# A first attention product in pairs of heads on two row groups of the matmul array

## The chip, the cores and the metric

The kernel runs on one core of a Trainium2 chip. A core has five engines that run their own instruction streams in order: TensorE (PE, matmuls, with its weight loads shown apart as PEld), VectorE (DVE), ScalarE (ACT), GpSimd (POOL) and SyncE (SP), which here issues nearly all loads and stores. Matmuls write to PSUM, eight banks of 2 KB a partition; the other data lie in SBUF, 128 partitions wide. The metric is the device time of one execution in microseconds (us). Before the change it is 344.74 us, the median of three runs (344.7 to 345.59).

## The reference: what is computed

Inputs are q, k, v and an output gate (4 batches, 8 heads, 768 steps, head size 40), an input and a forget gate (4, 8, 768), and weights of a feed-forward block. The first part is a recurrence over time with a decaying state:

```python
for t in range(S):
    m_new = np.maximum(f_gate[:, :, t] + m, i_gate[:, :, t])
    f_stab = np.exp(f_gate[:, :, t] + m - m_new)
    i_stab = np.exp(i_gate[:, :, t] - m_new)
    m = m_new
    C = f_stab[:, :, None, None] * C + i_stab[:, :, None, None] * np.einsum('bhd,bhe->bhde', vt, kt)
    n = f_stab[:, :, None] * n + i_stab[:, :, None] * kt
    h_tilde = np.einsum('bhde,bhe->bhd', C, qt)
    denom = np.maximum(np.abs(nq), 1.0)          # nq = n . q
    y[:, :, t] = o * h_tilde / denom             # o = sigmoid(o_gate)
```

The second part takes y with its heads side by side (4, 768, 320), multiplies by `w_in` (320 to 1024), applies ReLU, a convolution of width 3 over time for each of the 1024 channels, gates the result with its own sigmoid, and multiplies by `w_out` (1024 to 320). Results are f32.

## The kernel before, in words

**Tiling.** Time is cut into chunks of 128 steps: 6 a batch, 24 in all (`s`). Two chunks make a unit of 256 steps: 12 in all (`u`). Inside a chunk the recurrence is written as attention: a first product k.q for every head (128 x 128, "pS"), times a matrix of decay factors (`w`, an exp on ScalarE; `ch_p` multiplies on VectorE), then a second product with v (`ch_pv`, into "pY", 41 columns a head: 40 values and a one for the denominator). What earlier chunks hand on is a state matrix, updated by `ch_u` and `ch_state` and applied by `ch_inter`. The quotient and the gate give x (`ch_rden`, `ch_num`, `ch_x`), which is transposed on TensorE (`ch_t`) and split into a high and a low f32r part (`ch_split`, `ch_splitl`).

**Feed-forward block (FFN).** For each unit and each of 8 slices of the 1024 channels, 8 matmuls of 258 columns into "ph" (`f_m1`, line 618), ReLU, three taps, tanh and split on ScalarE, VectorE and GpSimd, and 6 matmuls of 320 columns into "po" (`f_m2`, line 681). Weights arrive as 64-bit numbers; `wabs`, `wc0` to `wc3`, `wsh` and `wsl` turn them into f32r pairs during the first part of the run.

**The first product before (`ch_s`, line 464).** Heads are kept in three groups of 3, 3 and 2, one above the other on partitions 0 to 119 (`q`, 40 a head). The stationary operand of head n is a tile `kz` of 120 partitions in which only that head's 40 are not zero; a matmul over 120 rows (80 in the last group) then gives that head's product. `kz` exists twice, is zeroed once by GpSimd (line 367), and a unit's loads (`att_kz`, lines 371 and 375) fill only the parts that are not zero: one load for q, three for k. Four heads fill one PSUM bank; the two banks of a chunk are two jobs, `s0` and `s1`. The pool `ps_m` (tag "m") has three banks, which `s0`, `s1`, `u` (state update), `t` (transposes) and the early gate transposes share in turn. The tile `q` is also read by `att_qe` on GpSimd or VectorE, which makes the operand of `ch_inter`.

**What sets the order.** Nothing is scheduled by the compiler. The kernel lists its pieces as jobs (`at(...)`) with what they come after, a cost on each engine (`COST`), a priority (place in the program plus an offset in `OFF`, `WZ`, `WL`), an earliest time for loads (`REL`, `SLOPE`), and a ring of buffers. The function `order` runs through this plan once while the program is built, always taking the job that could start first by those costs, and the jobs are written out in that order; each engine then follows its own part of it. Where the plan leaves TensorE idle early on, `warm` matmuls ("pw") fill the gap so that its clock stays up. On the chip only semaphores and the order on each engine count.

**Decay factors of the first three chunks** (`NP = 3`, `ch_gpe`, lines 405 and 408) are made on TensorE, by a 128-row matmul of 512 columns and four 32-row matmuls for each half of a chunk; later chunks load them (`ch_loadw`).

## Time and profile before

| what | before |
|---|---|
| median of three runs | 344.74 us |
| the profiled execution | 344.72 us |
| its span, first to last instruction | 342.6 us |
| TensorE busy | 328.7 us (96%) |
| weight loads busy | 322.3 us (94%) |
| VectorE busy | 262.9 us (77%) |
| ScalarE busy | 236.3 us (69%) |
| GpSimd busy | 202.7 us (59%) |
| line 464, the first product | 384 passes, 53.1 us busy, 287 ns the mean of one |
| bytes moved by DMA | 46.09 MB |
| mean granted clock of TensorE | 0.959 |

A pass of the first product lasts 287 ns, but passes overlap, so the busy time of a group is shorter than the sum of its durations: 384 passes in 53.1 us. In a timeline the distance between the starts of two groups tells what a group takes of TensorE. A line of the stretches view gives a stretch, its length, the busy time (and instructions) of each engine, the granted clock, the mean share of the 16 DMA engines that is busy, and GB/s. A waits row gives who waited for whom, in total, how often, and the longest. KB in the sizes of loads are 1024 bytes.

### The profile page before, as it was taken

To read this page: it belongs to the slowest core of one execution; us is meant where nothing else is said; L and a number is where in the kernel's file an instruction comes from. 1 tells how busy PE (TensorE), PEld (TensorE's weight loads), DVE (VectorE), ACT (ScalarE), POOL (GpSimd) and SP (SyncE) were. 2 spreads that over 40 slices of the span, in tenths; PEclk is the share of its full clock that TensorE was granted. 3 is DMA by queue.
4 is the path that set the end of the run, shared out by engine and by line. 5 is a ranking of instruction groups with operands and counts; after the bars stand their busy time and mean duration, and the time that the engine had idled before them with its cause. 6 is when DMAs were issued, how large, how long until landed. Compare 5 with 4: busy or idle time off the path is not lost.

```text
span 342.6 us, 7422 instructions
## 1 busy us (share of the span) xinstructions
PE 328.7 (96%) x2534; PEld 322.3 (94%) x2534; DVE 262.9 (77%) x598; ACT 236.3 (69%) x610; POOL 202.7 (59%) x310
## 2 busy tenths in 40 slices
PE   7699898998999999999999999999999999999995
PEld 7588898999999999999999999999999999999995
DVE  4897889999998987778489877676888768566750
ACT  2355747879988668896958786769685536577871
POOL 7369898869968647584745661746563234343341
PEclk9855599999999999999999999999999999999999
DMA  6887658686717466174315452654211001010111
GB/s 167 273 250 299 215 196 271 192 256 180 221 53 219 150 194 205 64 216 157 101 58 153 127 160 93 187 182 147 94 59 41 0 2 38 2 38 2 38 41 38
DMA packets 18575, 46.09 MB, mean 135 GB/s; under 512 B 2579, under 2 KB 6347, under 8 KB 18539
## 3 DMA queue, kind: packets, MB, share of 16 engines
q1 hardware_dynamic: 18068, 45.22, 42.4%
q8 instruction: 20, 0.33, 0.5%
q10 hardware_dynamic: 471, 0.41, 0.4%
q14 instruction: 16, 0.13, 0.1%
HBM read 41.49 MB, written 4.13 MB: 133 GB/s over the span
## 4 chain that ended last, share of the span: by engine, by line
PE 71%; DVE 11%; POOL 6%; ACT 4%; DMA 3%; issue 3%; SPq 0%; POOLq 0%; DVEq 0%; ACTq 0%
PE po L681 22%; PE ph L618 22%; PE pY L491 10%; PE pS L464 9%; PE pY L482 3%; PE pU L502 3%; PE pT L575 2%; DMA wraw<-in_w_in 1%; DVE cv L650 1%; DVE ph L650 1%; ACT w L439 1%; DMA w<-G_d 1%; PE pg L408 1%; POOL gl L209 1%; POOL w L432 1%
## 5 line engine op out<-in xcount | busy, mean ns | idle before, releaser
L209 POOL TENSOR_TENSOR gl<-cv,gh 128x512 fp32r<-128x512 f32 x48 | 62.5, 1302 | 47.4 <-ACT gh L213 40.7
L618 PE MATMUL ph<-X,wi_h 128*128 128x258 f32 x480 | 77.1, 290 | 2.2 <-DVE cv L650 1.5
L618 PEld LDWEIGHTS ph<-X,wi_h 128*128 128x128 f32 x480 | 64.6, 190 | 3.0 <-ACT ph L636 1.7
L681 PE MATMUL po<-wo_h,gh 128*128 128x320 f32 x192 | 61.5, 320 | 0.5 <-ACT ot L687 0.5
L439 ACT ACTIVATE w<-w,aT 128x128 f32<-128x128 f32 x168 | 55.1, 391 | 8.1 <-POOL w L432 8.1
L650 DVE SCALAR_TENSOR_TENSOR ph<-h,cw_sb,ph 128x256 f32<-128x256 f32 x96 | 46.1, 483 | 18.9 <-ACT ph L636 18.4
L681 PE MATMUL po<-wo_l,gh 128*128 128x320 f32 x192 | 59.3, 309 | 0.0
L681 PE MATMUL po<-wo_h,gl 128*128 128x320 f32 x192 | 59.3, 309 | 0.0
L464 PE MATMUL pS<-q,kz 120*128 120x128 f32 (+1 forms) x384 | 53.1, 287 | 4.2 <-DVE aT L306 3.1
L464 PEld LDWEIGHTS pS<-q,kz 120*128 120x128 f32 (+1 forms) x384 | 48.6, 199 | 4.6 <-DVE aT L306 3.2
L658 DVE SCALAR_TENSOR_TENSOR cv<-cv,h 128x512 f32<-128x512 f32 x48 | 40.4, 844 | 15.9 <-ACT cv L654 15.6
L628 ACT ACTIVATE h<-ph 128x258 f32<-128x258 f32 x96 | 36.5, 380 | 23.1 <-PE ph L618 21.2
L650 DVE SCALAR_TENSOR_TENSOR cv<-h,cw_sb,ph 128x256 f32<-128x256 f32 x96 | 45.1, 476 | 8.1 <-POOL gl L209 4.9
L618 PE MATMUL ph<-X,wi_l 128*128 128x258 f32 x288 | 50.3, 283 | 0.0
L491 PE MATMUL pY<-n,w 128*128 128x41 f32 x384 | 47.8, 282 | 0.0
L491 PEld LDWEIGHTS pY<-n,w 128*128 128x128 f32 x384 | 47.2, 197 | 0.2
L636 ACT ACTIVATE ph<-h,cw_sb 128x256 f32<-128x256 f32 x96 | 45.6, 475 | 1.9
L654 ACT ACTIVATE cv<-cv 128x512 f32<-128x512 f32 x48 | 30.1, 627 | 16.3 <-DVE cv L650 9.3
L618 PEld LDWEIGHTS ph<-X,wi_l 128*128 128x128 f32 x288 | 41.3, 190 | 0.0
L213 ACT ACTIVATE gh<-cv 128x512 fp32r<-128x512 f32 x48 | 30.0, 624 | 11.2 <-PE po L681 11.2
L681 PEld LDWEIGHTS po<-wo_h,gh 128*128 128x128 f32 x192 | 36.2, 188 | 0.7 <-ACT ot L687 0.7
L681 PEld LDWEIGHTS po<-wo_l,gh 128*128 128x128 f32 x192 | 36.2, 189 | 0.0
(84 smaller groups left out, 530.0 us busy)
## 6 DMA issues: line engine op xcount, KB each, us to landing
n<-in_nat SPq DMA_DIRECT2D x24, 484.0 KB
w<-G_d SPq DMA_DIRECT2D x21, 512.0 KB
q<-in_qT SPq DMA_DIRECT2D x12, 360.0 KB
out<-ot SPq DMA_DIRECT2D x24, 160.0 KB
wraw<-in_w_in SPq DMA_DIRECT2D x8, 384.0 KB
kz<-in_kT SPq DMA_DIRECT2D x24, 120.0 KB
eq<-E_d SPq DMA_DIRECT2D x24, 120.0 KB
wraw<-in_w_out SPq DMA_DIRECT2D x8, 320.0 KB
```

The source lines that it names most:

```text
L209: (nc.gpsimd if e == "POOL" else nc.vector).tensor_tensor(out=out, in0=in0, in1=in1, op=op)
L213: nc.scalar.activation(out, in_, AF.Copy)
L439: nc.scalar.activation(w[:, h, :], g, AF.Exp, bias=aT[:, c, b * 8 + h : b * 8 + h + 1])
L464: nc.tensor.matmul(pS[:, j, :], lhsT=lhsT, rhs=rhs, start=(j == 0), stop=(j == 3), skip_group_check=True)
L491: nc.tensor.matmul(pY[:, h * VW : (h + 1) * VW], lhsT=r["w"][:, n, :], rhs=v[:, DM + h * VW : DM + (h + 1) * VW], start=(c == 0 and n == 0 ...
L618: nc.tensor.matmul(ph, lhsT=a, rhs=b_, start=(i == 0), stop=(i == len(mm) - 1))
L628: nc.scalar.activation(hj, ph, AF.Relu)
L636: nc.scalar.activation(c, hk, AF.Copy, scale=wk)
L650: nc.vector.scalar_tensor_tensor(o, hk, wk, c, op0=ALU.mult, op1=ALU.add)
L654: nc.scalar.activation(cv, cv, AF.Tanh, scale=0.5)
L658: nc.vector.scalar_tensor_tensor(cv, cv, 1.0, h[:, :, 1 : 1 + UT], op0=ALU.add, op1=ALU.mult)
L681: nc.tensor.matmul(obuf[u][k], lhsT=a, rhs=b_, start=(f == 0 and i == 0), stop=(f == 7 and i == 2))
```

## The change

The first product of a chunk becomes one job `s` of eight matmuls. Two new arrays `qP` and `kP` hold q and k with heads 0 to 3 on partitions 0 to 39 and heads 4 to 7 on partitions 64 to 103 (the rows between are zeros from the host), four heads side by side along the free dimension. Matmul j of the lower half reads partitions 0 to 39 and writes bank `pS0`; matmul j of the upper half follows it, reads partitions 64 to 103 and writes bank `pS1`. The built program places the first kind as a tile of 64 rows at row 0 of the array and the second at row 64; before, all eight were tiles of 128 rows. The products are the same, over 40 rows instead of 120 of which 80 were zeros.

Loads of a unit: `k2` and `q2` (104 x 1024 each) and `q` as before (for `att_qe`), three loads instead of four, each into a ring of three tiles instead of two fixed `kz` tiles. The zeroing of `kz` and the wait of a unit's loads for the products of two units earlier go. One job takes two `m` banks, so `order` learns of a second list of users (`users2`). The table's cost of `s` is 1.15 where `s0` and `s1` had 0.86 each; `kz` keeps its cost of 1.5 and 2.2. All offsets in `OFF`, `WZ`, `WL`, `REL` and the numbers `SLOPE` and `QMAX` are different, so the whole order of the program is another.

```diff
-    cb=374.33, s0=-143.64, s1=77.22, p0=75.42, p1=778.82, inter=-156.65, pv0=139.58, pv1=72.13, rd0=-530.16,
+    cb=332.26, s=-382.2, p0=452.72, p1=1119.87, inter=28.33, pv0=86.13, pv1=-160.67, rd0=-659.34, rd1=-395.01,
...
-    ... cb={"POOL": 1.0, "DVE": 0.5}, s0={"PE": 0.86}, s1={"PE": 0.86}, p0={"DVE": 0.61}, p1={"DVE": 0.61},
+    ... cb={"POOL": 1.0, "DVE": 0.5}, s={"PE": 1.15}, p0={"DVE": 0.61}, p1={"DVE": 0.61},
...
-REL = dict(kz=-49.15, loadn=9.51, loadw=-633.44, eg=1.3)
-SLOPE = 2.41
-QMAX = 3.0
+REL = dict(kz=-326.94, loadn=22.7, loadw=-299.53, eg=5.25)
+SLOPE = 2.32
+QMAX = 2.88
...
-                        us = rings[r][k]
+                    us = list(rings[r][k]) if k >= 0 else []
+                    if j["users2"] and k >= -1:
+                        us += rings[r][k + 1]
+                    if us:
...
-    kzt = [const.tile([120, H, UT], F32, name=f"kz{k}") for k in range(2)]
-    for t in kzt:
-        nc.gpsimd.memset(t, 0.0)
-
     def att_kz(u):
-        q = sb.tile([120, 3 * UT], F32, name="q", tag="q", bufs=3)
-        nc.sync.dma_start(out=q, in_=qT[u])
-        kz = kzt[u % 2]
-        for j in range(3):
-            ng = 3 if j < 2 else 2
-            nc.sync.dma_start(
-                out=kz[40 * j : 40 * j + 40, 3 * j : 3 * j + ng, :],
-                in_=kT[u, 40 * j : 40 * j + 40, 0 : ng * UT],
-            )
-        units.setdefault(u, {}).update(kz=kz, q=q)
+        r = units.setdefault(u, {})
+        for nm, src, rows in (("k2", kP, 104), ("q2", qP, 104), ("q", qT, 120)):
+            t = sb.tile([rows, src.shape[2]], F32, name=nm, tag=nm, bufs=3)
+            nc.sync.dma_start(out=t, in_=src[u])
+            r[nm] = t
...
-    def ch_s(s, half):
+    def ch_s(s):
         u, tt = s // 2, (s % 2) * P
         r, ur = chunks[s], units[u]
-        pS = ps_m.tile([P, 4, P], F32, name="pS", tag="m")
+        for half in range(2):
+            r["s", half] = ps_m.tile([P, 4, P], F32, name=f"pS{half}", tag="m")
         for j in range(4):
-            n = 4 * half + j
-            g = n % 3
-            kk = 40 * GRP[g][1]
-            lhsT, rhs = ur["kz"][0:kk, n, tt : tt + P], ur["q"][0:kk, g * UT + tt : g * UT + tt + P]
-            nc.tensor.matmul(pS[:, j, :], lhsT=lhsT, rhs=rhs,
-                             start=(j == 0), stop=(j == 3), skip_group_check=True)
-        r["s", half] = pS
+            for half in range(2):
+                k, q = (ur[x][64 * half : 64 * half + D, j * UT + tt : j * UT + tt + P] for x in ("k2", "q2"))
+                nc.tensor.matmul(r["s", half][:, j, :], lhsT=k, rhs=q, start=(j == 0), stop=(j == 3), skip_group_check=True)
...
-        at("kz", z, [] if u < 2 else [(f"s{k}", 2 * (u - 2) + d) for d in (0, 1) for k in (0, 1)], att_kz, u, ring="q", users=ss + qe)
+        at("kz", z, (), att_kz, u, ring="q", users=ss + qe)
...
+        at("s", z, [("kz", u)] + ([("t", s - 2)] if s > 1 else []) + ([("u", s - 1 - (s - 1) // NCB)] if c else []), ch_s, s, ring="m", users=[("p0", s)], users2=[("p1", s)])
         for k in range(2):
-            at(f"s{k}", z, qk + ([("t", s - 2)] if s > 1 else []) + ([("u", s - 1 - (s - 1) // NCB)] if c else []), ch_s, s, k, ring="m", users=[(f"p{k}", s)])
-            at(f"p{k}", z, [(f"s{k}", s), ("exp", 4 * s + 2 * k), ("exp", 4 * s + 2 * k + 1)], ch_p, s, k)
+            at(f"p{k}", z, [("s", s), ("exp", 4 * s + 2 * k), ("exp", 4 * s + 2 * k + 1)], ch_p, s, k)
...
+    def pairs(x):
+        t = np.zeros((B, 3, 104, 4, UT), np.float32)
+        y = np.asarray(x)[:, HP].transpose(0, 1, 3, 2).reshape(B, H, D, 3, UT).transpose(0, 3, 2, 1, 4)
+        t[:, :, :D], t[:, :, 64:] = y[:, :, :, :4], y[:, :, :, 4:]
+        return t.reshape(B * 3, 104, 4 * UT)
```

Where the order differs, three places. First the loads on SP before the change, from the first unit's to the first `n` (the chunk's k, v and gate in natural layout):

```order
L371 DMA q<-in_qT 120x768
L375 DMA kz_107<-in_kT 40x768 x2
L375 DMA kz_107<-in_kT 40x512
L321 DMA wraw<-in_w_in 128x768
L289 DMA G_d<-Gt 32x128
L280 DMA E_d<-ft 32x128
L371 DMA q<-in_qT 120x768
L375 DMA kz_108<-in_kT 40x768 x2
L375 DMA kz_108<-in_kT 40x512
L321 DMA wraw<-in_w_in 128x768
L427 DMA n<-in_nat 128x968
```

and in the change, after the first two units' three loads each and one weight slice, up to the first `n`:

```order
L373 DMA q<-in_qT 120x768
L325 DMA wraw<-in_w_in 128x768
L382 DMA eq<-E_d 40x768 x2
L382 DMA eq<-E_d 40x512
L373 DMA k_202<-in_kP 104x1024
L373 DMA q_204<-in_qP 104x1024
L373 DMA q<-in_qT 120x768
L293 DMA G_d<-Gt 32x4x128
L286 DMA E_d<-ft 32x2x256
L325 DMA wraw<-in_w_in 128x768 x2
L422 DMA n<-in_nat 128x968
```

Two units stood ahead of the first `n`, now three do; the fourth stands ahead of the third `n`.

Second, TensorE before, up to the first FFN matmuls ("ph"); "pw" are the warm matmuls:

```order
L575 MATMUL pT<-id_sb,x 128x128 x3
L464 MATMUL pS<-q,kz_108 128x128 x8
L482 MATMUL pY<-cb,eq 128x123 x2
L482 MATMUL pY<-cb,eq 128x82
L491 MATMUL pY<-n,w 128x41 x8
L575 MATMUL pT<-id_sb,x 128x128 x3
L464 MATMUL pS<-q,kz_107 128x128 x8
L358 MATMUL pw<-wz 128x128 x2
L502 MATMUL pU<-n,wk 120x123 x2
L502 MATMUL pU<-n,wk 80x82
L358 MATMUL pw<-wz 128x128
L618 MATMUL ph<-X,wi_h 128x258 x5
```

and the same place in the change, where the eight rows of a first product alternate between two banks (two of them are shown below as the order has them):

```order
L458 MATMUL pS_623<-q_165,k_163 128x128
L458 MATMUL pS_624<-q_165,k_163 128x128
...
L567 MATMUL pT<-id_sb,x 128x128 x3
L474 MATMUL pY<-cb,eq 128x123 x2
L474 MATMUL pY<-cb,eq 128x82
L483 MATMUL pY<-n,w 128x41 x8
L610 MATMUL ph<-X,wi_h 128x258 x5
```

Ahead of the first "ph" stood five first products and five `u`; now four first products and three `u` do.

Third, later on TensorE, before the change, where the two halves of a chunk's first product are two jobs with FFN work between:

```order
L464 MATMUL pS<-q,kz_107 128x128 x4
L618 MATMUL ph<-X,wi_h 128x258 x5
L618 MATMUL ph<-X,wi_l 128x258 x3
L482 MATMUL pY<-cb,eq 128x123 x2
L482 MATMUL pY<-cb,eq 128x82
```

In the change all eight of a chunk stand in a row everywhere.

More of the change, by code (lines that the diff above doesn't have):

```diff
@@ L196, in tile_mlstm_ffn @@
 @with_exitstack
-def tile_mlstm_ffn(ctx, tc, fg, ig, qT, kT, nat, w_in, w_out, cw, msk, tr, out):
+def tile_mlstm_ffn(ctx, tc, fg, ig, qT, qP, kP, nat, w_in, w_out, cw, msk, tr, out):
     nc = tc.nc
@@ L701, in tile_mlstm_ffn, with at @@
     seen = {}
-    def at(key, z, after, fn, *a, ring=None, users=(), cost=None):
+    def at(key, z, after, fn, *a, ring=None, users=(), users2=None, cost=None):
         n = seen[key] = seen.get(key, -1) + 1
@@ L707, in at @@
             after = list(after) + [(key, n - 1)]
-        jobs[key, n] = dict(cost=COST[key] if cost is None else {eng: cost}, z=round(z + OFF[key], 2), rel=REL[key] + SLOPE * z if key in REL else 0.0, after=after, ring=ring, users=users, fn=fn, a=a)
+        jobs[key, n] = dict(cost=COST[key] if cost is None else {eng: cost}, z=round(z + OFF[key], 2), rel=REL[key] + SLOPE * z if key in REL else 0.0, after=after, ring=ring, users=users, users2=users2, fn=fn, a=a)
     def weight(i, key, src, n, *dst):
@@ L819, in tile_mlstm_ffn @@
         j["fn"](*(([j["eng"]] if len(COST[e[0]]) > 1 else []) + list(j["a"])))
-_INS = ["fg", "ig", "qT", "kT", "nat", "w_in", "w_out", "cw", "msk", "tr"]
+_INS = ["fg", "ig", "qT", "qP", "kP", "nat", "w_in", "w_out", "cw", "msk", "tr"]
 def kernel(**inputs):
@@ L854 @@
         "qT": heads(q),
-        "kT": heads(k),
+        "qP": pairs(q),
+        "kP": pairs(k),
         "nat": nat,
```

28 lines of the change are left out of this document (14 added, 14 removed).

## The prediction

> **What bounds the kernel now.** I read the page first: busy shares, the slices, the chain that ended last.
>
> ```profile
> span 342.6 us, 7422 instructions
> PE 328.7 (96%) x2534; PEld 322.3 (94%) x2534; DVE 262.9 (77%) x598; ACT 236.3 (69%) x610; POOL 202.7 (59%) x310
> ...
> PEclk9855599999999999999999999999999999999999
> DMA  6887658686717466174315452654211001010111
> ...
> PE 71%; DVE 11%; POOL 6%; ACT 4%; DMA 3%; issue 3%; SPq 0%; POOLq 0%; DVEq 0%; ACTq 0%
> ```
>
> TensorE is busy nearly throughout and carries 71% of the chain, but a share is a mean over stages. So next come the busy times by stretch, for all engines and then for the first product (line 464) alone.
>
> ```profile
> 0.00:60.00 60.00, 52.51 (x312) 47.92 (x313) 48.87 (x105) 31.51 (x94) 46.54 (x75) 0.77 0.77 239
> 60.00:120.00 60.00, 58.41 (x494) 57.58 (x492) 57.51 (x140) 50.04 (x143) 46.58 (x72) 1.00 0.60 181
> 120.00:300.00 180.00, 179.71 (x1458) 179.43 (x1458) 134.55 (x315) 127.58 (x317) 95.34 (x153) 1.00 0.35 108
> 300.00:342.60 42.60, 38.08 (x278) 37.32 (x277) 21.97 (x41) 27.18 (x59) 14.21 (x11) 0.99 0.09 32
> ...
> 60.00:120.00 60.00, 12.78 (x96) 11.63 (x96) 1.00 0.60 181
> 120.00:300.00 180.00, 27.18 (x208) 24.96 (x208) 1.00 0.35 108
> ```
>
> The columns are PE, PEld, DVE, ACT, POOL, then clock, DMA share and GB/s (the last two rows: PE and PEld of line 464). There are three stages. To 60 us nobody is full: loads are heavy (share 0.77), the clock is partly at half, and PE's busy time contains idle-filling products. From 60 to 120 us PE and VectorE are both full (57.51 of 60 us): VectorE still converts weights. From 120 to 300 us PE alone is full (179.71 of 180 us; VectorE 75%). A microsecond of PE work saved there is a microsecond of time; between 60 and 120 us VectorE lets through only part of it. Line 464 has 208 records in the third stage, which at 16 a chunk is 13 chunks, and 6 chunks in the second.
>
> **What the eight matmuls cost now.**
>
> ```profile
> 212.82 1.99 PE L464 MATMUL pS<-q,kz 120*128 120x128 f32 x16
> 214.64 0.49 PE L575 MATMUL pT<-id_sb,x 128*128 128x128 f32 x3
> ...
> 206.78 0.98 PE L491 MATMUL pY<-n,w 128*128 128x41 f32 x8
> 207.59 0.84 PE L618 MATMUL ph<-X,wi_h 128*128 128x258 f32 x5
> ```
>
> Each f32 matmul is two passes (a weight load and a stream each). From start to the next group's start a chunk takes 214.64 - 212.82 = 1.82 us, or 114 ns a pass. The second product streams only 41 columns, yet takes (207.59 - 206.78)/8 = 101 ns a pass: at that length something other than the stream, most likely the load of 128 columns of weights, sets the pace.
>
> **What they will cost.** No row shows two row groups at work together, so I bound it. Below: every pass runs beside one of the other group, 1.82/2 = 0.91 us. Above: streams overlap but weight loads follow one another, 16 x 0.101 = 1.62 us. To both comes the change of shape: the new matmuls use 64 rows of the array, their neighbours 128. For that there is a row, the decay product of the start, which alternates 128-row and 32-row matmuls at full clock:
>
> ```profile
> 201.59 0.31 PE L681 MATMUL po<-wo_l,gh 128*128 128x320 f32 x1
> 201.74 0.31 PE L681 MATMUL po<-wo_h,gl 128*128 128x320 f32 x1
> ...
> 8.43 1.15 PE L408 MATMUL pg<-Gt,id_sb 32*128 32x128 f32 x8
> 9.51 0.51 PE L405 MATMUL pg<-tri 128*128 128x512 f32 x1
> 9.94 1.15 PE L408 MATMUL pg<-Gt,id_sb 32*128 32x128 f32 x8
> 10.94 0.19 PE L300 MATMUL pt<-id_sb,rst 32*128 32x32 f32 x1
> ```
>
> A 320-column pass takes 0.15 us, so 512 columns should take 0.24; with a change to 32 rows behind it, it takes 9.94 - 9.51 = 0.43, so entering costs 0.19. Eight 32-row passes take 9.51 - 8.43 = 1.08 us when 128 rows follow and 10.94 - 9.94 = 1.00 when 32 rows follow, so leaving costs 0.08. Together 0.27 us a chunk. That gives 1.18 us at the lower and 1.89 us at the upper bound. I take the lower, 1.18: the pairs share no array rows, no partitions and no PSUM bank, the one thing they may share is the way the weights come in, and PEld's rows do not show whether that way or the array's rows make the 101 ns. Saved: 0.64 us a chunk.
>
> [...]
>
> **Third stage.** 13 chunks x 0.64 = 8.3 us saved.
>
> **Loads and the start.** The sizes, and the places in the trace:
>
> ```profile
> q<-in_qT SPq DMA_DIRECT2D x12, 360.0 KB
> kz<-in_kT SPq DMA_DIRECT2D x24, 120.0 KB
> kz<-in_kT SPq DMA_DIRECT2D x12, 80.0 KB
> ...
> 22.98 0.68 SPq L427 DMA_DIRECT2D n<-in_nat  x1
> ...
> 59.90 0.85 PE L618 MATMUL ph<-X,wi_h 128*128 128x258 f32 x5
> ...
> 45.51 0.64 PE pU L502 x6
> ...
> 49.03 1.75 PE pY L491 x16
> 50.78 0.35 PE pT L575 x3
> ...
> 52.92 0.63 PE pY L482 x6
> ```
>
> A unit was 360 + 2 x 120 + 80 = 680 KB in four loads; it becomes 2 x 416 (104 x 1024 x 4 bytes) + 360 = 1192 KB in three. 512 KB more, at 239/0.77 = 310 GB/s, is 1.7 us of wire a unit, 20 us in all, while `kz` keeps its planned 2.2 us. SP issues 12 loads fewer and skips the wait for its zeroing, which gates the first k load:
>
> ```profile
> 1.75 1.76 POOL kz L367
> ...
> 3.53 0.30 SPq L375
> ```
>
> That gives back under 2 us at the very start. But the order now puts three units ahead of the first `n` and a fourth ahead of the third. Up to and with the third `n` load I count 11,985 KB against 6,465 KB: 12.3 MB, which is 40 us at 310 GB/s and 51 us at the mean 239. In the trace that load is issued at 22.98 us, its chunk's second product runs at 49.03, the first FFN matmul at 59.90. From that second product to the first FFN matmul the new order has 6.6 us of PE work, by the chain's rows: 1.75 for it, 1.75 + 0.63 for the next chunk's with `inter`, 1.18 for one first product, 0.64 for a `u`, 2 x 0.35 for two transposes. With the loads starting at about 2 us, the first FFN matmul can start between 48 and 60 us; I take 55, five earlier than now, since the order needs one first product and two `u` fewer before it. Past 60 us the DMA share falls to 0.60 and 0.35: seven units x 1.7 us over 280 us add four points, hidden; with that cover gone each would cost 1.7 us.
>
> **Second stage.** 5 us of earlier start and 6 x 0.64 = 3.8 us are 8.8 us of possible gain, but VectorE keeps its work and has 60 - 57.51 = 2.5 us free there. Its queue goes on as before, so what is late next is the conversion of the w_out halves and the taps behind them. I take 3.0 of the 8.8; bounds 0 and 8.8.
>
> **PSUM, POOL, end.**
>
> ```profile
> L471 DVE TENSOR_TENSOR w<-w,pS 128x512 f32<-128x512 f32 x48 | 32.5, 680 | 4.1 <-PE pS L464 3.5
> L367 POOL MEMSET kz<- 120x2048 f32 x2 | 3.5, 1804 | 0.0
> ...
> 326.53 0.98 PE ph L618 x8
> 327.54 0.40 ACT h L628
> ...
> 331.57 6.88 PE po L681 x45
> ```
>
> A chunk now needs two of three `m` banks at once; its second pair waits for a bank that the pending product (DVE, line 471), `u` or `t` still holds. Behind that wait stand the FFN matmuls. VectorE's readers of these products stood idle only 4.1 us in all, so the order keeps them apart from the products by other work; I take 0 and bound it by one read of a bank for each chunk, 24 x 0.68 = 16 us, far off, as the order puts other work between. The two memsets (3.5 us on POOL) go, beside other work: 0. At the end 8 groups of second FFN matmuls instead of 11 follow the last first one. Between that one's relu (327.54) and the last 45 passes (331.57) lie 4.0 us, which the three groups more (a group is 6 passes, 6 x 6.88/45 = 0.92 us) helped to fill: 2.8 us less of cover, of which I take 0.8 (bounds 0 and 2.8), near the lower end because that stretch was not full before either (PE 38.08 busy of 42.6 us from 300 us on).
>
> **Sum.** -8.3 - 3.0 + 0.8 = -10.5 us. The profiled execution took 344.72 us (2.1 around its span), as good as the median 344.74. So 344.7 - 10.5 = 334.2 us.
>
> **Rivals.**
> *The loads take the early gain.* For: three units ahead of the first `n`, share 0.77 already, and the plan counts a unit as short as before. Against: a quarter of the wire is free. With the first FFN matmul at 60 us and w_out late by two units (3.4 us): -8.3 + 0.8 + 3.4 - 0.6 (part of the second stage) = -4.7, 340 us.
> *No price for changing shape.* If loads of the 64-row groups run ahead through the change, 0.91 us a chunk: 13 x 0.91 = 11.8, 4.2 in place of 3.0 in the second stage, 0.8 at the end: -15.2, 329.5 us. Against: the 0.19 us above.
> *Weight loads do not pair: slower.* Then a chunk takes 1.89 us; the mechanism decides as soon as it exceeds 1.82. All 24 chunks lose 0.07 (1.7 us), the plan starts everything behind a chunk too early, the loads cost 1.7 us for each of the units ahead of the third `n` less what was free (about 3 us), and the end 0.8: 350 us. For it: 101 ns a pass with a short stream. Against: row groups are separate rows of the array. [...]
> *The change is not what it says.* The built program gives the eight a 64-row tile at row 0 or 64, so this is left out.
>
> **How the numbers follow.** Forecast (331 to 337.5) 0.52; loads take the early gain (338 to 343) 0.19; no price for the shape (327 to 331) 0.13; loads in a line (344 to 353) 0.16. A measurement tells 0.3%, 1.0 us, from no change. Faster: the first three but for the edge at 343 to 344, 0.82; same 0.04; slower 0.14. The range holds 8 in 10 from 329 (leaving 0.06 below, inside the third case) to 343 (leaving 0.14).
>
> **What would show it.** In the profile after: groups of 16 passes of line 458 at 1.1 to 1.3 us start to start (0.9 or 1.9 point to the rivals), with a gap of about 0.2 us ahead of their first weight load; the first FFN matmul at 52 to 58 us; DMA share above 0.85 to 60 us; VectorE above 95% until 110 us; PE still full from 120 us. Waits of FFN matmuls for line 471, or PE idle for `n` or `wraw` loads past 60 us, would prove the sum wrong.

## The result and the profile after

The changed kernel takes 361.9 us (median of four, 356.89 to 366.06) against 344.96 us (four runs, 344.7 to 345.59): slower, ratio 1.04 [1.03, 1.05], which is 0.04 x 345 = 13.8 us. The forecast was 334.2 us in a range of 329 to 343. Some runs are disturbed, so ratios here are of undisturbed runs alone, and where a kernel has no ratio all of its runs are given.

From the page of the changed kernel (profiled execution 360.81 us, span 358.8 us):

```profile
PE 330.8 (92%) x2554; PEld 316.0 (88%) x2554; DVE 260.8 (73%) x601; ACT 231.8 (65%) x609; POOL 198.5 (55%) x306
...
PEclk9655558599999989999999999999999999999999
...
PE 43%; DMA 19%; ACT 11%; DVE 10%; POOL 7%; issue 6%; SPq 1%; POOLq 0%; ACTq 0%; DVEq 0%
```

TensorE's share of the chain falls from 71 to 43%, and DMA's rises from 3 to 19%. The clock is at half in slices 3 to 6, comes up in the 7th and is at half once more in the 8th (a slice is 9 us). The stretches of the same kernel (PE, PEld, DVE, ACT, POOL, clock, DMA share, GB/s):

```profile
0.00:60.00 60.00, 49.14 (x263) 44.03 (x264) 38.97 (x84) 25.57 (x75) 31.91 (x55) 0.63 0.77 225
60.00:120.00 60.00, 52.99 (x431) 50.06 (x431) 55.35 (x129) 44.44 (x124) 43.58 (x68) 0.91 0.69 213
120.00:300.00 180.00, 173.58 (x1432) 168.20 (x1432) 127.04 (x305) 125.51 (x331) 104.02 (x166) 0.99 0.45 137
```

To 60 us there are 263 matmul records instead of 312 and the clock is 0.63 instead of 0.77; from 120 us on, TensorE has 6.4 us idle where it had 0.3. The timeline of TensorE in the changed kernel (start, length, and so on):

```profile
57.12 1.92 PE L483 MATMUL pY<-n,w 128*128 128x41 f32 x16
...
60.99 1.13 PE L458 MATMUL pS<-q,k 40*128 40x128 f32 x14 [0.62 <-DVE X L582]
63.74 0.90 PE L567 MATMUL pT<-id_sb,x 128*128 128x128 f32 x3 [1.62 <-DVE x L546]
...
66.77 3.64 PE L483 MATMUL pY<-n,w 128*128 128x41 f32 x16 [0.92 <-DVE w L463]
70.20 1.42 PE L610 MATMUL ph<-X,wi_h 128*128 128x258 f32 x5
...
209.59 0.73 PE L494 MATMUL pU<-n,wk 128*120 128x123 f32 x6
210.25 1.16 PE L458 MATMUL pS<-q,k 40*128 40x128 f32 x16
211.34 0.42 PE L673 MATMUL po<-wo_h,gh 128*128 128x320 f32 x1
```

A group ahead of the product in the kernel before:

```profile
185.46 0.73 PE L502 MATMUL pU<-n,wk 128*120 128x123 f32 x6
186.03 1.09 PE L464 MATMUL pS<-q,kz 120*128 120x128 f32 x8
```

The pairs do what they should: 211.34 - 210.25 = 1.09 us a chunk instead of 1.66 to 1.83 (the chunks of before between 127 and 290 us, the two halves added where they stand apart), and `pU` ahead of them takes 210.25 - 209.59 = 0.66 us instead of 0.57. But the first FFN matmul starts at 70.20 us instead of 59.90. So the question is not why the product failed, but what ate its gain and 14 us besides.

A queue and the chain already name a suspect. The issues of SyncE in the changed kernel, and below them pieces of its chain of waits in order of time (start, length, what):

```profile
106.20 0.34 SPq L373 DMA_DIRECT2D k<-in_kP  x1
106.58 0.37 SPq L373 DMA_DIRECT2D q<-in_qP  x1
107.05 0.33 SPq L373 DMA_DIRECT2D q<-in_qT  x1
111.05 0.35 SPq L413 DMA_DIRECT2D w<-G_d  x1
111.45 0.42 SPq L422 DMA_DIRECT2D n<-in_nat  x1
```

```profile
19.24 8.58 DMA wraw<-in_w_in
...
52.33 4.32 PE pw L362 x22
...
111.45 7.12 DMA n<-in_nat
...
121.12 7.50 DMA n<-in_nat
...
156.96 7.89 DMA eq<-E_d
...
181.91 7.92 DMA n<-in_nat
...
218.50 8.74 DMA n<-in_nat
```

A unit's three loads (1192 KB) stand on the queue ahead of the `w` (512 KB) and the `n` (484 KB) that the next chunk waits for. Five loads of `n` and `eq` lie on the chain for 7.1 to 8.7 us each, long past 60 us. Four of them are issued 0.4 to 4.4 us behind the last of a unit's three; behind the one at 121.12 us the next unit's three follow 2 us later. In e1 below, the same order with 680 KB a unit, the chain past 60 us has one such load (6.78 us).

The late first FFN matmul is less simple. Between 27.8 us (19.24 + 8.58) and 111.45 us no load lies on the chain. From 43 to 59 us it is TensorE's own work, up to 56 us at half clock, and 4.32 us of it are 22 passes of warm matmuls, which compute nothing.

### The profile page after: what moved, and what is told of

Same layout as the page of the kernel before. It is cut to its first block, busy times and chain, and to the rows that moved or that the text cites. A ratio compares the mean times of both kernels' runs of the same rounds, so it can differ in the third digit from the quotient of the medians.

```text
span 358.8 us, 7412 instructions
## 1 busy us (share of the span) xinstructions
PE 330.8 (92%) x2554; PEld 316.0 (88%) x2554; DVE 260.8 (73%) x601; ACT 231.8 (65%) x609; POOL 198.5 (55%) x306
## 4 chain that ended last, share of the span: by engine, by line
PE 43%; DMA 19%; ACT 11%; DVE 10%; POOL 7%; issue 6%; SPq 1%; POOLq 0%; ACTq 0%; DVEq 0%
PE ph L610 13%; PE po L673 12%; DMA n<-in_nat 9%; PE pY L483 7%; DMA eq<-E_d 5%; PE pS L458 4%; ACT w L434 3%; DMA wraw<-in_w_in 2%; ACT ph L628 2%; PE pY L474 2%; PE pU L494 2%; DVE cv L642 2%; POOL eq L213 2%; DVE ph L642 2%; ACT gh L217 2%
## 5 line engine op out<-in xcount | busy, mean ns | idle before, releaser
L610 PE MATMUL ph<-X,wi_h 128*128 128x258 f32 x480 | 78.8, 295 | 8.5 <-DVE cv L642 3.6
L610 PEld LDWEIGHTS ph<-X,wi_h 128*128 128x128 f32 x480 | 65.8, 193 | 12.7 <-issue 3.5
L434 ACT ACTIVATE w<-w,aT 128x128 f32<-128x128 f32 x168 | 56.0, 393 | 15.7 <-POOL w L427 15.7
L483 PE MATMUL pY<-n,w 128*128 128x41 f32 x384 | 51.1, 297 | 1.8 <-DVE w L463 0.9
L483 PEld LDWEIGHTS pY<-n,w 128*128 128x128 f32 x384 | 49.9, 209 | 2.9 <-issue 1.2
L650 DVE SCALAR_TENSOR_TENSOR cv<-cv,h 128x512 f32<-128x512 f32 x48 | 35.4, 737 | 12.3 <-ACT cv L646 11.8
L673 PEld LDWEIGHTS po<-wo_h,gl 128*128 128x128 f32 x192 | 36.1, 188 | 0.6 <-POOL gl L213 0.6
L458 PE MATMUL pS<-q,k 40*128 40x128 f32 x384 | 32.7, 308 | 2.7 <-DVE aT L310 2.1
L463 DVE TENSOR_TENSOR w<-w,pS 128x512 f32<-128x512 f32 x48 | 31.9, 680 | 4.3 <-ACT w L434 2.9
```

What stands on the lines that cost most here:

```text
L434: nc.scalar.activation(w[:, h, :], g, AF.Exp, bias=aT[:, c, b * 8 + h : b * 8 + h + 1])
L458: nc.tensor.matmul(r["s", half][:, j, :], lhsT=k, rhs=q, start=(j == 0), stop=(j == 3), skip_group_check=True)
L463: nc.vector.tensor_tensor(w, w, r["s", half], op=ALU.mult)
L483: nc.tensor.matmul(pY[:, h * VW : (h + 1) * VW], lhsT=r["w"][:, n, :], rhs=v[:, DM + h * VW : DM + (h + 1) * VW], start=(c == 0 and n == 0 ...
L610: nc.tensor.matmul(ph, lhsT=a, rhs=b_, start=(i == 0), stop=(i == len(mm) - 1))
L650: nc.vector.scalar_tensor_tensor(cv, cv, 1.0, h[:, :, 1 : 1 + UT], op0=ALU.add, op1=ALU.mult)
```

## The experiments

Two words for what follows. The "old order" is the order of jobs that the plan of before gives; the "new order" is that of the changed kernel (other offsets, one job `s`). "Half clock" is time in the first 100 us at half the clock, worked out from the mean clock of that stretch as (1 - clock) x 200 us: 28 us before and 54 us after, by these rows of the stretches view (the clock is the third number from the end; before first):

```profile
0.00:100.00 100.00, 91.62 (x644) 86.61 (x645) 87.78 (x202) 66.03 (x192) 78.22 (x121) 0.86 0.71 216
```

```profile
0.00:100.00 100.00, 82.30 (x523) 75.33 (x524) 76.98 (x169) 53.86 (x153) 60.49 (x101) 0.73 0.76 227
```

### Is it the pairs, the order or the bytes?

**e1: the new order with the product of before.** Line 464's product and the four loads of 680 KB, in the order of the change.

```diff
-    k, q = (ur[x][64 * half : 64 * half + D, ...] for x in ("k2", "q2"))
+    lhsT, rhs = ur["kz"][0:kk, n, tt : tt + P], ur["q"][0:kk, g * UT + tt : g * UT + tt + P]
```

> The change's order of jobs, but the first product and its loads as before the change: 128-row matmuls with the zeroed tiles (three of them instead of two), four loads of 680 KB a unit instead of three of 1192 KB. A chunk's first product should take 1.8 us again instead of 1.1. Theory A (the longer loads of a unit arrive late and everything behind them waits): the first FFN matmul comes back from 70 us to 60 to 63 us, and in spite of some 24 x 0.7 = 17 us more TensorE work the time is 344 to 353 us, below the change's 361. Rival B (the new order of jobs is itself a bad one, whatever is loaded): the first FFN matmul stays at 68 us or later and the time is 361 to 375 us. Rival C (the 64-row shape disturbs TensorE and its clock): TensorE's clock from 40 to 70 us returns to 0.95 or more, which A also allows, but the loads' share to 60 us would stay what it was.

Measured: 350.96 us, ratio 1.017 [1.011, 1.022]; half clock 34 us, first FFN matmul at 63.42 us. The order alone (with the one job of sixteen passes that belongs to it), without pairs and without one byte more, costs 5.7 us (0.0166 x 344.8; the interval allows 4 to 7.5).

**e2: the change with k2 and q2 of unit 0 for all units** (the first product of the other units is then of the wrong data; some 430 KB a unit).

```diff
...
+            if u and nm != "q":
+                r[nm] = units[0][nm]
+                continue
```

> The change with its pairs and its order, but the two new tiles are loaded for the first unit alone and read by all units (so the first product of the other eleven units is computed from the first unit's q and k, and those results are left wrong). 832 KB a unit fall away for eleven units; a unit's load is then 360 KB. Theory A: the first FFN matmul at 55 to 61 us, the time 328 to 338 us, since pairs then save their 0.6 to 0.7 us a chunk. Rival B (the order): first FFN matmul at 67 us or later, time above 350 us. Rival C (the 64-row shape disturbs TensorE or its clock): time above 350 us and the clock from 40 to 70 us still at 0.6 to 0.75, as the shape is unchanged.

Measured: 342.3, 342.84, 350.73 and 354.68 us, median 346.78. With fewer bytes the same order and the same pairs are level with before, and 15 us faster than the change by the medians. The 328 to 338 us of theory A were not reached, so the bytes are not the whole loss.

**e3: the kernel before with 512 KB more a unit** (zeros that nobody reads).

```diff
+        more = sb.tile([P, 4 * UT], F32, name="more", tag="more", bufs=2)
+        nc.sync.dma_start(out=more, in_=xtra[u])
```

> The kernel before, with its own order and product, plus one load of 512 KB a unit behind that unit's four loads, into a tile that nothing reads. That is the change's additional volume and nothing else. Theory A: 5 to 15 us slower (350 to 360 us), first FFN matmul at 63 us or later. Rivals B and C: within 2 us of 345, as the order and the shape are those of before.

Measured: 347.92 us, ratio 1.010 [1.008, 1.012], first FFN matmul at 63.37 us. In the old order 512 KB more cost 3.4 us, less than theory A said (5 to 15) and more than its rivals (2). Nothing reads this load; where the loads are read, in e11 and e12 below, 312 KB make 0.010 x 344.8 = 3.4 us. So bytes have no fixed price: it depends on the order and on what waits for them.

**e4: the change with the halves in turn** (all lower heads, then all upper ones).

```diff
-        for j in range(4):
-            for half in range(2):
+        for half in range(2):
+            for j in range(4):
```

> The change with the two loops of the first product swapped: the four matmuls of the lower row group in a row, then the four of the upper one. The same work, loads and order otherwise. If pairs overlap only when neighbours lie in different row groups, a chunk takes 1.8 to 1.9 us again instead of 1.1 and the time rises by 5 to 15 us. If 64-row tiles are faster for another reason (fewer rows), it stays at 1.1 us and the time at 361 us. Theories A, B and C agree here; it measures what the alternation alone is worth.

Measured: 370.61 us, ratio 1.076 [1.071, 1.081]. TensorE in e4:

```profile
214.20 1.71 PE L458 MATMUL pS<-q,k 40*128 40x128 f32 x16
215.84 0.41 PE L673 MATMUL po<-wo_h,gh 128*128 128x320 f32 x1
```

The same sixteen passes take 215.84 - 214.20 = 1.64 us when their row groups do not alternate, so the 1.09 us of the change come from two groups at work together. 24 x (1.64 - 1.09) = 13.2 us, and the kernel got 0.036 x 344.8 = 12.3 us slower (the intervals allow some 8 to 16). In the new order a microsecond of this product is worth about a microsecond of time.

**e6: no padding rows** (two loads of 40 rows for k2, two for q2; 1000 KB a unit in five loads).

```diff
...
+                for p in (0, 64):
+                    nc.sync.dma_start(out=t[p : p + D, :], in_=src[u, p : p + D, :])
```

> The change with the 24 rows of zeros between the two row groups no longer loaded: two loads of 160 KB for each of the two tiles instead of one of 416 KB, so a unit is 1000 KB in five loads instead of 1192 KB in three, in the change's order. Results are the same. If volume in this order is what costs (the 832 KB that the run with one unit's q and k left out were worth 361 - 347 = 14 us), 192 KB less should give about 192/832 of that, 3 us (356 to 360 us), less up to 1 us for the two more issues of a unit. If the time does not fall, the number of loads, not their volume, decides.

Measured: 355.55 us, ratio 1.031 [1.028, 1.034]: 192 KB a unit less give about 3 us by the ratios (0.0086 x 344.8).

**e7: k2 and q2 loaded for units 0 to 3 only** (the later units use unit 3's, so their first product is wrong).

```diff
+            if u > 3 and nm != "q":
+                r[nm] = units[3][nm]
+                continue
```

> The change with its order, but the two new tiles are loaded for units 0 to 3 alone, as in the change; units 4 to 11 read those of unit 3 (their first products are computed from its q and k, and those results are left wrong). The start is then loaded as in the change, the middle of the run with 832 KB less a unit. Theory A in its present form (loads of n, w and eq stand behind a unit's loads in one queue and land 7 to 8 us after their issue, at the start and in the middle): the first FFN matmul stays at 68 to 71 us, the waits of 7 to 8 us for n loads between 110 and 220 us shrink to 3 to 5 us, and the time falls to 350 to 355 us, that is by about the 9 us by which the part behind the first FFN matmul is shorter in the run with one unit's q and k. If only the start matters (rival D: all of the loss is the late first FFN matmul and the clock at half before it), the time stays at 358 to 362 us.

Measured: 350.45 us, ratio 1.013 [1.006, 1.020], the time as expected. The bytes of units 4 to 11 are worth 0.027 x 344.8 = 9.3 us (the intervals allow some 5 to 13): they were not hidden. The first FFN matmul starts at 65.86 us, not at the 68 to 71 expected, although both kernels issue the same loads up to 55 us. So one profile gives this start to within some 4 us, no better.

### Can the plan be told the price?

**e5: the change with the plan's cost of a unit's loads raised to what 1192 KB take** (2.2 to 3.86 us of wire, the issue lowered from 1.5 to 1.2), the offsets kept.

```diff
-    kz={"SP": (1.5, 2.2)}, ...
+    kz={"SP": (1.2, 3.86)}, ...
```

> The change, its pairs, loads and offsets, with one line of the table altered: a unit's loads are counted as 3.86 us of wire (1192 KB at the 310 GB/s of the early stretch) and 1.2 us of issue instead of 2.2 and 1.5. The order is made anew from that. If the loss comes from loads that the order counted too short (theory A, as mended: not the volume by itself, since 512 KB more cost only 3 us in the old order, but the new order's tight placing of the loads behind a unit's loads), the waits of 7 to 8 us for n loads between 110 and 200 us disappear from the chain and the time falls to 344 to 354 us; the first FFN matmul stays late (64 us or more), since the volume is the same. If the order of the other jobs is what is bad (rival B), the time stays at 357 us or more, since the offsets are the same.

Measured: 370.56 us, ratio 1.075 [1.069, 1.080]. Missed: the first FFN matmul moved to 65.04 us, but its chain still has an `eq` load of 8.98 us and `n` loads of 7.56 and 6.47 us. That offsets found for one set of costs are no good for another fits this, but is not shown by it.

**e9 and e10: offsets sought anew**, by trying offsets against the plan's own forecast. e9 has the pairs with 880 KB a unit (as e6, and three heads of the lower half read from `q`); e10 is the kernel before, with nothing but its offsets, early load times and queue depth replaced.

First e9's product (its offsets, and the plan's costs of loads and product, change too), then one line of e10:

```diff
-                k, q = (... for x in ("k2", "q2"))
+                qs = "q" if half == 0 and j < 3 else "q2"
+                k, q = (... for x in ("k2", qs))
```

```diff
-    gpe=-466.23, loadw=661.3, mask=-269.35, ...
+OFF = dict(gpe=-1768.09, loadw=1400.17, mask=-695.46, ...
```

> Pairs with fewer bytes: the rows of zeros are not loaded, and three of the four lower heads are read from the tile q, where they already lie on partitions 0 to 39; a unit is 880 KB in five loads. All offsets are sought anew with 3.1 us of wire and 1.9 us of issue a unit, as in the run above. Theory A: 330 to 339 us, faster than the kernel before by 6 to 14 us. Rival C: 350 us or more.

> The kernel before with its own product and loads, and offsets sought anew in the same way. It tells what the search by itself is worth. Theory A: 341 to 347 us, within 1% of before, so that a gain of the two runs with pairs is that of the pairs. If it also comes to 335 us, the search and not the pairs made the gain.

Measured: e9 349.7 us, 1.015 [1.013, 1.017]; e10 353.12 us, 1.028 [1.024, 1.032]. Both missed. The seeking itself costs the kernel before 9.5 us, so e9 says nothing against pairs: under the same seeking, pairs with 880 KB are 0.013 x 344.8 = 4.4 us faster than the product of before. That is one sought order of each, so the 4.4 us may as well be the luck of the seeking as the pairs. The same seeking with the change's 1192 KB (e8) was not measured.

### The pairs in the old order

**e11 and e12: the order of before, the pairs at the place of `s0`,** with 1192 KB (e11) and 880 KB a unit (e12).

```diff
+    def ch_s(s, part):
+        if part != 0:
+            return
```

e12 loads 880 KB in five loads on top of that (and reads three lower heads from `q`, as e9 does):

```diff
-            nc.sync.dma_start(out=t, in_=src[u])
...
+                c = 3 * UT if nm == "q2" else 0
+                nc.sync.dma_start(out=t[0:D, c:], in_=src[u, 0:D, c:])
+                nc.sync.dma_start(out=t[64:104, :], in_=src[u, 64:104, :])
```

> The kernel before with its own offsets, costs and so its own order of jobs; only the product and its loads are the change's: all eight matmuls, in pairs, at the place where the first four stood, and three loads of 1192 KB a unit at the place of the four of 680 KB. No zeroing. Theory A': the pairs save about 0.7 us a chunk wherever TensorE is full, 19 chunks x 0.7 = 13 us, the additional volume costs about 3 us in this order (as the run with 512 KB more did), so 333 to 338 us; the change's loss is then its new order, with the loads that stand tight in it. Rival A (the volume costs in any order): 350 us or more. Rival C (the 64-row shape costs elsewhere): 345 us or more, with first FFN matmul at 60 us.

> As the run above, but with 880 KB a unit in five loads (no rows of zeros; three of the lower heads read from the tile q). Theory A': 1 to 3 us faster than the run above, 331 to 337 us. If the number of loads costs more than their volume, it is slower than the run above.

**e13: e12 with the halves in turn,** as e4 is to the change.

> As the run with 880 KB a unit in the old order, but the four matmuls of the lower row group in a row and then the four of the upper one. A chunk should take 1.64 us, as halves in turn did in the change's order, instead of 1.09. Theory A': 0.55 us a chunk on 19 chunks, so 8 to 12 us slower than the pairs, 341 to 347 us. If the pairs' gain is hidden by another engine, within 3 us of the pairs.

Measured: e11 364.56 us, 1.054 [1.048, 1.060]; e12 359.69 us, 1.044 [1.041, 1.047]; e13 361.39 us, 1.048 [1.040, 1.056]. The theory that the new order is the only culprit falls with e11, which missed by 27 us. And e13 is level with e12: here the pace of the product buys little (1.4 us, and by the intervals no more than some 4). A part of the reason shows in the timeline of e18 (below; also the old order with pairs):

```profile
197.46 0.48 PE L459 MATMUL pS<-q,k 40*128 40x128 f32 x2
198.43 1.16 PE L459 MATMUL pS<-q,k 40*128 40x128 f32 x14 [0.48 <-DVE Cst L508]
199.51 0.75 PE L611 MATMUL ph<-X,wi_h 128*128 128x258 f32 x4
```

The two passes of the first matmul, into the first bank, start; the second bank is still held by the state update's reader (`Cst`), and the other fourteen passes wait: 199.51 - 197.46 = 2.05 us a chunk, more than the 1.7 us of before. In e12 four of the ten chunks between 150 and 290 us wait like this, five take 1.09 us. In e13 three of the chunks at these places take 2.05 us too, pairs or not, and the fourth 4.07 (3.17 in e12); the others take 1.64. Over these ten chunks e12 is still 3.6 us ahead (16.5 against 20.1 us); where the kernel loses that again was not traced.

### Is it the clock?

By then a pattern stood out: kernels with 40-row products had 40 to 62 us at half clock, those with 120 rows 24 to 34. Windows of e3 and of e12 at about the same place (stretch, length, PE, PEld, DVE, ACT, POOL, clock, DMA share, GB/s):

```profile
41.39:44.80 3.41, 3.41 (x17) 3.21 (x17) 3.17 (x8) 2.54 (x9) 3.41 (x7) 0.53 0.64 137
44.81:48.20 3.39, 3.39 (x33) 3.39 (x33) 2.29 (x6) 3.20 (x12) 3.39 (x4) 1.00 0.84 269
```

```profile
41.65:45.06 3.41, 3.41 (x23) 3.19 (x21) 2.23 (x5) 1.98 (x6) 3.41 (x7) 0.50 0.79 205
45.07:48.48 3.41, 3.41 (x25) 3.04 (x23) 2.98 (x5) 2.66 (x10) 2.58 (x3) 0.50 0.60 193
```

By the profile TensorE is busy all through the first window in both, with products, one `u` and three passes of `inter`. Behind e3's (120-row products) the clock is full; behind e12's (40-row pairs) it stays at half. The theory: narrow products do not lift the clock, and half clock is the loss. One thing spoke against rows as the whole cause: from 49.74 us on e12 runs some 5 us of 128-row passes without a gap (seven passes of 41 columns, then `pU` and warm ones), still at half pace. Two `pU` in there take 1.22 us (52.45 - 51.23) and 1.09 us (54.05 - 52.96), where the kernel before has 0.57 at full clock. The windows are 3.41 us long, a step that the clock itself shows: in the changed kernel it goes up at 55.95 us, down at 62.78 and up at 73.02, two and three times 3.41 us apart.

**e14 and e17: four full-height matmuls that compute nothing behind the product,** in chunks 0 to 5 of e12 (e14) and in chunks 0 to 3 of the change (e17).

```diff
+        if s < 6:
+            warm(4)
```

> e12 (the order of before, pairs, 880 KB a unit: 359.69 us, some 48 us of its first 100 at half clock) with four warm matmuls of 128 rows behind the product of chunks 0 to 5, so 24 matmuls that compute nothing. Theory C (products of 40 rows do not hold TensorE's granted clock up): half clock falls to 27 to 38 us, first FFN matmul at 60 to 64 us instead of 67.8, 345 to 353 us, though the 24 matmuls cost 2.6 us at full clock and 5 at half. Rival D (the clock only follows from waits for loads and PSUM banks): half clock stays at 45 us or more, 358 to 364 us.

> The change (361.9 us, 58 us at half clock, first FFN matmul at 70.2 us) with four warm matmuls behind the product of chunks 0 to 3. Theory C: half clock 30 to 45 us, first FFN matmul at 62 to 67 us, 348 to 357 us. Rival D: half clock 52 us or more, 360 to 366 us.

Measured: e14 365.18, 362.08, 369.77 and 369.32 us with 44 us at half clock (clock 0.78); e17 360.57, 362.15, 352.02 and 359.13 us with 54 us (0.73) in the profiled run of 360.57 us. e14 missed: it is slower than both expectations in three of four runs. e17 is unclear: two runs and the profiled clock are as rival D said, one run (352.02 us) is as theory C said. In e14 the first rise did come 10 us earlier (the clock is 0.55 from 41.84 to 45.24 us and 1.00 from 45.25 to 48.66 us, while e12's passes come to full pace at about 55 us), but the clock fell again. Two windows of e14 about a fall:

```profile
69.15:72.55 3.40, 1.29 (x10) 1.32 (x10) 1.93 (x5) 0.51 (x2) 0.29 (x1) 0.95 0.33 100
72.56:75.96 3.40, 3.40 (x18) 3.40 (x17) 0.49 (x1) 2.02 (x6) 2.56 (x3) 0.50 0.00 0
```

TensorE was busy only 1.29 of 3.4 us before the fall, waiting for VectorE's last tap. So here half clock followed a wait for late work, and the windows filled early did not help the later ones.

**e15: pairs over all 64 rows of a group** (24 rows of zeros more, 1384 KB a unit, otherwise e11).

```diff
-    ur[x][64 * half : 64 * half + D, ...]
+    ur[x][64 * half : 64 * half + 64, ...]
```

> e11 (the order of before, pairs, whole rows: 364.56 us, 1192 KB a unit) with 64 rows in each matmul instead of 40, the added 24 being zeros from the host (1384 KB a unit). If the rows that a matmul reads decide the clock: half clock 35 to 48 us instead of 54.6 and 352 to 360 us. If the tile of 64 rows as such does it, or neither: half clock 52 us or more, and the 192 KB more a unit make it 364 to 370 us.

Measured: 362.44, 363.62, 358.59 and 352.27 us, half clock 52 us (0.74) in the profiled run of 362.44 us. Its clock speaks against the rows that are read as the cause. Of the times, two lie in the range that speaks for them (352 to 360) and two between the ranges; the fastest has a mean clock of 0.95 over the whole run, the profiled one 0.918, and no profile shows where. Inconclusive.

**e16: the product of before in chunks 0 to 5, pairs with 880 KB from chunk 6 on,** in the old order.

```diff
+        if u >= 3:
+            return att_k2(u)
...
+        if s < 6:
+            return ch_s1(s, part)
```

> e12 with the product of before (120 rows, 680 KB a unit) in chunks 0 to 5, the pairs from chunk 6 on (880 KB a unit). Theory C: half clock 24 to 31 us as before, first FFN matmul at 59 to 62 us, and the pairs then gain up to 18 x 0.6 us: 335 to 345 us. Rival D (what costs is the bytes and waits of the later units): 349 to 357 us.

Measured: 356.61 us, ratio 1.031 [1.023, 1.039], half clock 30 us (0.85), first FFN matmul at 63.87 us. The clock of the start is back, and with it 4.5 us of the 15 that e12 lost (0.013 and 0.044 x 344.8), although six chunks have the slower product again. So half clock can be a part of the loss, but not the whole: 335 to 345 us were expected if it were, and e16 is in the range of the rival, the bytes and waits of the later units. Among what is left are the waits at the places of the old order, and one more, seen in VectorE's timeline of e16:

```profile
33.05 0.35 DVE L339 TENSOR_SCALAR wf<-wmag 128x384 int32<-128x384 int32 x1
...
34.91 4.00 DVE L339 TENSOR_SCALAR wf<-wmag 128x384 int32<-128x384 int32 x1
```

The same instruction takes 0.35 and then 4.00 us; GpSimd runs several groups one behind the other meanwhile (last section). The reader of a transpose stands behind it, and the product waits for that, by the waits of e16 (the same wait is 1.09 us in the kernel before):

```profile
PE pS L476 <- DVE X L616: 4.6, 1, 4.6
```

### The two missing corners

**e18: pairs in the old order (e11) with k2 and q2 of unit 0 only,** the edit of e2. **e19: the new order with the product of before (e1) and 520 KB of kz's zeros loaded as well,** 1200 KB a unit in three loads (640, 360 and 200 KB, where the change has 416, 416 and 360).

```diff
...
-                out=kz[40 * j : 40 * j + 40, 3 * j : 3 * j + ng, :],
-                in_=kT[u, 40 * j : 40 * j + 40, 0 : ng * UT],
+        nc.sync.dma_start(out=kz[0:80, :, :], in_=kT[u, 0:80, :, :])
+        nc.sync.dma_start(out=kz[80:120, 3:, :], in_=kT[u, 80:120, 3:, :])
```

> e11 (pairs at the places that s0 had in the order of before, 364.56 us) with k2 and q2 loaded for unit 0 only; all other units use unit 0's, so the first product is wrong for them. About 430 KB a unit are loaded, less than the 680 of before. If the bytes are the loss: 332 to 345 us. If the pairs do not suit the places of the old order (both PSUM banks at once, windows that no longer lift the clock): 350 to 360 us, since e3 showed only 3.1 us for 512 KB in this order.

> e1 (the order of the change, product of before over 120 rows, 350.96 us) with kz loaded with 520 KB of its zeros besides: 1200 KB a unit in three loads, where the change has 1192 in three. If the bytes are most of the loss in this order (e2 against the change: 15 us): 360 to 368 us, so that the pairs are worth up to 4 us at equal bytes. If the 64-row tiles are most of it (58 us at half clock against 27): 352 to 356 us and half clock below 35 us.

Measured: e18 358.87 us, 1.038 [1.034, 1.043]; e19 370.34 us, 1.071 [1.067, 1.075], half clock 52 us with a 120-row product. In the old order the bytes are the smaller part of the loss: e18 gives back 0.016 x 344.8 = 5.5 us of e11's 18.7. In the new order they are the larger part, and e19 lies 2 us above what was expected for that. And a 40-row product is not needed for a long half clock. The corners together (times, and ratios to the kernel before):

| order | product | KB a unit | ratio | time us |
|---|---|---|---|---|
| old | 120 rows | 680 | 1 | 344.7 to 345.0 |
| old | 120 rows | 1192 (e3) | 1.010 | 347.92 |
| old | pairs | about 430 (e18) | 1.038 | 358.87 |
| old | pairs | 1192 (e11) | 1.054 | 364.56 |
| new | 120 rows | 680 (e1) | 1.017 | 350.96 |
| new | 120 rows | 1200 (e19) | 1.071 | 370.34 |
| new | pairs | about 430 (e2) | none | 342.3 to 354.7 |
| new | pairs | 1192 (the change) | 1.04 | 361.9 |

Read along the new order: its places cost 5.7 us (e1), the bytes 18.6 us more (e19 against e1), and the pairs take back 0.031 x 344.8 = 10.7 us (the change against e19; the intervals allow some 7 to 14, and the loads are not of the same sizes). 5.7 + 18.6 - 10.7 = 13.6 us, the 1.04 of the change; the sum closes by itself, since its terms are differences along one path. Another path has other terms: with pairs and 1192 KB the new order is the faster one (1.04 against e11's 1.054). e4 gave 12.3 us for the alternation alone.

Where the bytes bite shows in the waits for DMA, in the order before, e3 (old order), e1, e19 (new order), all with 120-row products (who waited for what: us in total, times, longest):

```profile
POOL w L432 <- DMA w<-G_d: 5.7, 6, 1.3
ACT wmag L326 <- DMA wraw<-in_w_in: 5.2, 2, 3.6
POOL dcol L215 <- DMA eq<-E_d: 1.2, 1, 1.2
```

```profile
ACT wmag L326 <- DMA wraw<-in_w_in: 10.9, 3, 6.7
POOL w L434 <- DMA w<-G_d: 6.6, 6, 2.5
POOL dcol L215 <- DMA eq<-E_d: 1.8, 1, 1.8
```

```profile
POOL dcol L219 <- DMA eq<-E_d: 8.3, 3, 3.3
POOL w L436 <- DMA w<-G_d: 5.3, 4, 1.6
ACT wmag L330 <- DMA wraw<-in_w_in: 4.5, 4, 2.7
```

```profile
ACT wmag L330 <- DMA wraw<-in_w_in: 12.2, 3, 4.9
POOL dcol L219 <- DMA eq<-E_d: 11.9, 3, 5.3
POOL w L432 <- DMA w<-G_d: 11.3, 7, 4.7
```

In the old order the added bytes lengthen the waits for weight loads (5.2 to 10.9 us), and nothing waits long for `eq` (1.2 and 1.8). In the new order GpSimd waits 8.3 us for `eq`, on which the inter-chunk product hangs, with the bytes of before already: that is the order's doing. The bytes add there to all three, to the weight loads and `w` most. The three rows add up to 12.1 and 19.3 us in the old order, to 18.1 and 35.4 us in the new one. These are waits of engines, not all of them loss, but they grow as the times do.

No kernel of the study beat the kernel before with the right result. What stays open: why, beyond the waits for `eq`, the new offsets cost 5.7 us with the product of before, and how the 13 us of pairs in the old order divide between the wait for the second bank, late FFN taps and half clock. Other loads in the new order (880 KB without seeking offsets) were not tried.

## Why the prediction was wrong, step by step

- **Bounds of the stages.** Right about the kernel before. In the new order e4 moved the time by 12.3 us for 13.2 us of product, but TensorE is no longer full there: it is idle 6.4 us from 120 to 300 us.
- **The price of the pairs, 1.18 us.** Right in the sum, in part by luck. The group takes 1.09 us, and `pU` ahead of it 0.66 instead of 0.57 us: 1.18. But the change of shape was to cost 0.19 us on entering, and costs 0.09; and the group was to take 0.91 + 0.08 = 0.99 us, and takes 1.09. Taking the lower bound was right: sixteen passes take 1.64 us in turn (e4) and 1.09 in alternation, and in the changed kernel their sixteen weight loads are done in 0.97 us (PEld at 210.25 us), where loads in a line at the prediction's 101 ns would take 1.62. That speaks against weight loads in a line, which was weighed as a rival. That rival forecast the right sign for a reason that did not occur. "No price for changing shape" falls too, by 0.09 us.
- **"13 chunks x 0.64 = 8.3 us saved".** Near at equal bytes and order: 10.7 us for all 24 chunks by e19, where the sum had 8.3 + 3.0. The 0.64 is a little high: it takes the 1.82 us of one chunk, and twelve chunks of before between 127 and 290 us have a mean of 1.73, which leaves 0.55 us a chunk. In the time the gain does not show, for the next steps.
- **"The first FFN matmul ... I take 55, five earlier than now".** This failed: 70.20 us. The step summed bytes to the third `n` load and 6.6 us of TensorE work from its chunk's second product on, at full clock and without waits. That product starts at 57.12 us, where the step's own bounds give 41 to 53, and from there it takes 70.20 - 57.12 = 13.1 us: waits of 0.62, 1.62 and 0.92 us, and a last second product at half clock (70.20 - 66.77 = 3.43 us instead of 1.75). In e1, with the bytes of before in the new order, the same two are 51.09 and 12.3 us, so the 6.6 us were wrong without any added byte. The other 6 us, ahead of that product, go with the bytes and the pairs; the chain does not show how. e1 has the first FFN matmul at 63.42 us, e19 at 72.59 us, both in the new order; with e3 (63.37) the bytes alone cost 3.5 us in the old one. The upper end of the step, 60 us, had no row behind it for a clock that stays at half: 26 us more of half clock are up to 13 us of work. The rival "the loads take the early gain" named a mechanism that is a part of it, but priced it at 3.4 us and without any delay of the first FFN matmul.
- **"Four points, hidden".** This failed most. The added bytes cost 18.6 us in the new order (e19 against e1), and in the changed kernel those past unit 3 alone cost 9.3 us (e7). The mean DMA share (0.45 from 120 to 300 us) was indeed low; what counted, by the chain, was the queue, where 1192 KB stand ahead of or beside an `n` or `eq` that the next chunk needs. The step's own fallback, 1.7 us of wire a unit "with that cover gone", gives 7 x 1.7 = 12 us and would have been nearer.
- **The order itself.** It was given a price only at the start (gain) and at the end (0.8 us). Its places cost 5.7 us with the old product, a term that the sum lacked.
- **"PSUM ... I take 0".** Nearly right in the new order: behind the start, the wait of 0.62 us at 60.99 us is what there is. In the old order it would have been wrong: 2.05 us and more for four of ten chunks instead of 1.09.
- **What would show it.** Groups of 1.09 us fell just under "1.1 to 1.3"; "PE idle for `n` loads past 60 us" was named as what would prove the sum wrong, and the chain has it.

## What to carry to other kernels

A change that makes an engine's piece shorter and its operands larger has two prices, and the mean DMA share (0.45 here from 120 to 300 us) did not show the second: look on the queue for the load that the next step needs, and count what is newly ahead of it. In a kernel whose order was fitted to its costs, price the new order by itself (old work in the new places) and the new work in the old places before crediting either; the two need not add up. A product that needs two banks at once had its pace only where both were free (e18, 150 to 290 us: 1.09 us in five of ten chunks, 2.05 to 2.33 in the four that waited for the second bank).

## What the runs showed of the hardware

- Two row groups of 64 rows in alternation took 1.09 us for sixteen f32 passes (68 ns each; the change), in turn 1.64 us (103 ns; e4), and the 120-row form took 1.66 to 1.83 us (before). So the 64-row form by itself saved little here, and the rest came from two groups at work at once. Going from a 128-row group to these cost 0.09 us (`pU` 0.66 instead of 0.57 us, one place in each kernel).
- After 3.41 us in which TensorE is busy throughout the clock was full in e3 (41.39 us; 1.00 behind it) and at half in e12 (41.65 us; 0.50 behind it). Why was not settled; some 5 us of 128-row passes from 49.74 us on ran at half pace in e12 too. A low clock also followed idle time: in e14 1.29 of 3.40 us busy from 69.15 us, then 0.50; in the kernel before no matmul from 12.45 us, and 0.50 from 14.14 us on.
- In e16 the same VectorE instruction (line 339) took 0.35 us at 33.05 us and 4.00 us at 34.91 us. During the longer one GpSimd showed:

```profile
34.52 1.06 POOL L209 TENSOR_TENSOR eq<-eq,q 80x256 f32<-80x256 f32 x1
...
35.68 1.94 POOL L209 TENSOR_TENSOR wi_l<-wf,wi_h 128x384 fp32r<-128x384 f32 x2
37.58 1.08 POOL L444 TENSOR_SCALAR_AFFINE_SELECT w<-w 128x1024 f32<-128x1024 f32 x1
38.64 1.57 POOL L209 TENSOR_TENSOR wk<-n,wT 128x120 f32<-128x120 f32 x3
```

  It ended at 34.91 + 4.00 = 38.91 us, just behind the end of the group of L444 (37.58 + 1.08 = 38.66 us), while GpSimd went on with the next. In the changed kernel line 347 took 0.54 us at 34.83 us and 3.47 us at 38.95 us, the longer one beside the same GpSimd operation (L427, 39.43 to 40.52 us); GpSimd was busy throughout both. What made the long ones long is not shown.
- Some kernels with pairs vary more from run to run than the kernel before (the change 356.89 to 366.06 us, against 344.7 to 345.59), others do not (e6 355.18 to 356.04, e12 358.24 to 360.58). Why was not looked into.
